# First feed-forward group: weight pieces rebased ahead of the exponentials, key and value sums moved within the step, a weight round in step 8, whole products in four steps

## The chip, the cores and the metric

The kernel runs on one core of one Trainium2 chip. The metric is the device time of one execution in microseconds (us), the median over several runs. The core's engines run side by side and each works through its own queue in order: TensorE (PE, matmuls), VectorE (DVE), ScalarE (ACT), GpSimd (POOL) and SyncE (SP, which here only issues DMA transfers). An instruction that waits holds up all that stands behind it in the same queue.

## The reference

Attention with a window of 16 keys and 24 key blocks, each summed up by one key (the maximum over the block's 32 keys) and one value (their mean), and then a feed-forward layer on the result:

```python
def _attn_ref(q, k, v):                       # 4 batches, 8 heads, 768 tokens, 64 wide
    k_sum = k.reshape(B, H, nb, block, D).max(axis=3)
    v_sum = v.reshape(B, H, nb, block, D).mean(axis=3)
    scores_l = scale * np.matmul(q, k.transpose(0, 1, 3, 2))     # only |i - j| < 16 counts
    scores_s = scale * np.einsum('bhsd,bhnd->bhsn', q, k_sum) + np.log(block)
    scores_all = np.concatenate([np.where(mask_l, scores_l, -1e9), scores_s], axis=-1)
    a = softmax(scores_all)
    return np.matmul(a, np.concatenate([v, v_sum], axis=2))

def _moe_ref(x, w_in, w_out):                 # 3072 x 512, 512 x 2048, 2048 x 512
    h = x @ w_in
    g = h * np.tanh(np.log1p(np.exp(np.minimum(h, 20.0))))
    return g @ w_out
```

Weights arrive as 64-bit floats.

## The kernel before

The 3072 tokens are handled in 6 groups of 512. A *step* `i` of the main loop (line 559) is one group and one of 16 slices of 128 of the inner dimension: `ff_in` makes the slice (12 matmuls of 128x512 into `ph`), `ff_act` the activation on ACT, `ff_split` cuts it into a high part `ah` and a low part `al = a - ah`, and `ff_out` of the slice two steps earlier adds it to the output (12 matmuls into `po`). Each product is made of three: high times high, low times high, high times low. Steps 0 to 15 are the first group; in the first `WHOLE = 6` of them `ff_out` does one product of whole 32-bit values instead (line 469).

Attention for the next group is woven into these steps. The table `at` gives the steps in which the scores of a pair of (chunk, head pair) units are made: 0, 4, 8, 12, 15, 19 and so on. The scores of step 8 are thus prepared in steps 3 to 7. What follows them: DVE adds the mask and takes the minimum (`nm`, line 366), ACT takes the exponentials (line 370), DVE computes `rs`, POOL multiplies with it (line 384), three steps later PE transposes and one step after that multiplies with the values.

**Weights, first group only.** `w_in` and `w_out` are loaded in 16 pieces of two slices, numbered here by the order of loading (`w_in` 0; `w_in` 2, `w_out` 0; `w_in` 4, `w_out` 2; ...). Each goes through a round spread over several steps: `load_weight` issues two DMAs into one of two stage buffers, which come free when the piece two rounds earlier has been read; `begin_weight` has ACT rebase the 64-bit value's upper word into `f` (line 146) and DVE shift out the bits `x` (lines 150 and 152); `join_weight` has DVE clamp `f` and join both (lines 160 and 162); `upper_weight` casts the high part `w_hi` on ACT (line 178); `lower_weight` subtracts it on DVE, `w_lo` (line 185). In step `i` piece `i + 3` is joined and piece `i + 4` begun until step 7; step 8 leaves these out (line 622), and from step 9 on it is `i + 2` and `i + 3`. In the steps of `at` the rebase is put off to the next step (`begin_weight(i in at)`, line 624), where it stands in ACT's queue behind the exponentials. Pieces of `w_out` that serve whole products are cut after step 14.

**Sums.** For every new batch, and for each of two units `n` and `m` of a pair, the key source `ks` is loaded, DVE takes block maxima `km` (line 269), then the value source `vsum` is loaded into the same single buffer, and DVE sums it into `vq` (line 297), which SP stores as `vm`. POOL copies `km` into the query block `qk` (line 308) before the scores use it. In the first group this happens for the scores of steps 8 and 12.

Everything is emitted under a manual schedule: the order of the code is the order of each engine's queue.

Of the kernel before, what the change touches and what calls it, by code (L numbers as in the profile page):

```python
# [9 lines left out]
F32 = mybir.dt.float32  # L10
# [32 lines left out]
WP = 512  # L43
WB = 2
SQ = 32
WHOLE = 6


OFFSET = 112
# [10 lines left out]
def fused_kernel(ctx: ExitStack, tc: tile.TileContext, q0, qk, kt, v0, vw, vs, w_in, w_out, out):  # L60
# [48 lines left out]
    def home(j, part, dtype, name):  # L109

        if j == NW:
            t = stage.tile([P, WB, WP], I64, tag="stage", name=name).bitcast(dtype)
            return t.rearrange("p k f -> p (k f)")[:, :WB * WP]
        pool = const if j < EARLY else late[0]
        return pool.tile([P, WB * WP], dtype, tag=f"w{part}_{j}", name=name, bufs=1)

    def value_home(j, name):
        return home(j if j in whole else min(k for k in range(j + 1, NW + 1) if k not in whole), 1, F32, name)
# [1 line left out]
    def weight(w, part, fc):  # L120
        return split[w, fc - fc % WB, part][:, fc % WB * WP:(fc % WB + 1) * WP]

    loaded, rebases, begun, joined, raised, kept = [], [], [], [], [], []

    def load_weight():
        if weights:
# [4 lines left out]
            loaded.append((w, fc, t))  # L131

    def rebase_weight():
        if rebases:
            rebases.pop(0)()

    def begin_weight(wait=False):
        if loaded:
            w, fc, t = loaded.pop(0)
            j = order[w, fc]  # L140
            flat = t.rearrange("p k f -> p (k f)")
            high = flat.bitcast(U32).rearrange("p (f two) -> p f two", two=2)[:, :, 1]
            quarter = flat.bitcast(U16).rearrange("p (f four) -> p f four", four=4)
            x = home(j, 0, U32, f"x{w}_{fc}")
            f = value_home(j, f"f{w}_{fc}")
            rebases.append(lambda: nc.scalar.activation(f, high.bitcast(F32), AF.Copy, scale=2.0 ** -OFFSET))
            if not wait:
                rebase_weight()
            half = x.bitcast(U16).rearrange("p (f two) -> p f two", two=2)
            nc.vector.tensor_scalar(out=half[:, :, 0], in0=quarter[:, :, 1], scalar1=13, scalar2=None,  # L150
                                    op0=ALU.logical_shift_right)
            nc.vector.tensor_scalar(out=half[:, :, 1], in0=quarter[:, :, 3], scalar1=SIGN, scalar2=None,
                                    op0=ALU.bitwise_and)
            begun.append((w, fc, f, x))
# [15 lines left out]
    def upper_weight():  # L170
        if joined:
            w, fc, f = joined.pop(0)
            if order[w, fc] in whole:
                value = f
                f = home(NW, 1, F32, f"f{w}_{fc}")
                nc.scalar.copy(f, value)
            split[w, fc, 0] = home(order[w, fc], 0, F32R, f"w{w}_{fc}_hi")
            nc.scalar.copy(split[w, fc, 0], f)  # L178
            raised.append((w, fc, f))
# [136 lines left out]
    def att_summarize_values(c, hp):  # L316
        b, th = divmod(c, CPB)
        if th == 0:
            value_summary(b, hp)
# [113 lines left out]
    def ff_in(g, fc):  # L433
        xh, xl = xs[g]
        ph = ps_w.tile([P, TG], F32, tag="w", name=f"ph{g}_{fc}")
        wh, wl = (weight(0, part, fc) for part in range(2))
        for cc in range(NCC):
            for n, (w, x) in enumerate(((wh, xh), (wh, xl), (wl, xh))):
                nc.tensor.matmul(ph, w[:, cc * P:(cc + 1) * P], x[:, cc, :],  # L439
                                 start=(cc == 0 and n == 0), stop=(cc == NCC - 1 and n == 2))  # L440
        st[g, fc] = ph

    def ff_act(g, fc):

        if g == 0 and fc < WHOLE:
            a = ff.tile([P, TG], F32R, tag="ah", name=f"a{g}_{fc}").bitcast(F32)
        else:
            a = ff.tile([P, TG], F32, tag="t", name=f"a{g}_{fc}", bufs=2)
        nc.scalar.activation(a, st[g, fc], AF.Mish)  # L449
        st[g, fc] = a  # L450

    def ff_split(g, fc):

        if g == 0 and fc < WHOLE:
            return lambda: None
        a = st[g, fc]
        ah = ff.tile([P, TG], F32R, tag="ah", name=f"ah{g}_{fc}")
        al = ff.tile([P, TG], F32R, tag="al", name=f"al{g}_{fc}")

        (nc.scalar.copy if g == 0 else nc.vector.tensor_copy)(ah, a)  # L460
        st[g, fc] = ah, al
        return lambda: nc.vector.tensor_sub(al, a, ah.bitcast(F32))  # L462
# [93 lines left out]
    values = dict(zip(turns[1:] + [turns[-1] + 4], (at[i] for i in turns)))  # L556
    turned = {i + 3: group for i, group in at.items() if i < NFC - 1}
    following = dict(zip(turns, (at[i] for i in turns[1:])))
    for i in range(len(steps) + 2):
        if i - 1 in at and i < NFC:  # L560
            att_normalize(at[i - 1])
        if i < len(steps):
            ff_in(*steps[i])
            ff_act(*steps[i])
            if i < NFC:
                split_rest = ff_split(*steps[i])
            if i in turned:
                att_transpose(turned[i])
        if i - 1 in at:
            upper_weight()  # L570
            rebase_weight()
        if i < NFC and i - 1 in following:

            att_summarize_values(*following[i - 1][0])
        group = values.get(i)
        lower = att_values(group) if group else None
        if lower and i >= NFC:
            lower()
        if i in at:
            att_scores(at[i], i >= NFC - 1)  # L580
        if i < NFC:
            if lower:
                lower()
            split_rest()
        if i - 1 in at and i >= NFC:
            att_normalize(at[i - 1])
        if i - 3 in at and i - 3 >= NFC - 1:
            att_transpose_blocks(at[i - 3], 1)
        if NFC <= i < len(steps):
            ff_split(*steps[i])()  # L590
        if i - 2 in at and i - 2 >= NFC - 1:
            att_transpose_blocks(at[i - 2], 0)
        if i - 3 in following:
            n, m = following[i - 3]
            att_summarize_values(*m)
            after = todo.index(m) + 1
            if after < len(todo) and todo[after][0] % CPB == 0:
                load_key_source(todo[after][0] // CPB, todo[after][1])
        if i in following:
            n, m = following[i]  # L600
            att_summarize_keys(*n)
            if i >= NFC - 1:
                for unit in (n, m):
                    att_load_keys(*unit)
        if i - 1 in following:
            n, m = following[i - 1]
            if i >= NFC:
                att_summarize_values(*n)
            if m[0] % CPB == 0:
                load_key_source(m[0] // CPB, m[1])  # L610
            if i < NFC:
                for unit in (n, m):
                    att_load_keys(*unit)
        if i - 2 in following:
            n, m = following[i - 2]
            att_summarize_keys(*m)
            for unit in (n, m):
                att_block_keys(*unit)
        if i == NFC - 2:
            joined.extend(kept)  # L620
        if i not in at:
            upper_weight()
        if i != NFC // 2:
            join_weight()
            begin_weight(i in at)
            load_weight()
        if i not in at:
            lower_weight()
        if i - 1 in at:
            lower_weight()  # L630
        if group:
            for unit in at.get(i, ()):
                att_load_values(*unit)
        if i >= 2:
            ff_out(*steps[i - 2])


# [42 lines left out]
```

## Time and profile before

| | us |
|---|---|
| runs shown, median of 3 | 644.27 (639.81 to 644.44) |
| profiled execution, device time | 646.44 |
| its span, first to last instruction | 644.7 |
| PE busy | 612.1 (95%) |
| DVE, ACT, POOL busy | 382.2 (59%), 259.1 (40%), 76.3 (12%) |
| mean granted TensorE clock, share of full | 0.976 |

The first group's steps begin at 44.5 us, when PE starts `ff_in(0)`; before that comes the attention of the first 512 tokens. A page's row of digits cuts the span into 40 slices of 16.1 us. In rows of a timeline the first number is the start, the second the duration; neighbouring matmuls overlap, so the distance of their starts is what one costs. `w_8` alone can be the ninth slice pair of `w_in` or of `w_out`; which one is meant follows from its place.

### The profile page before, as it was taken

The page shows a single profiled execution, that of the slowest core. Times are in us where ns is not written, and L with a number is a line of the kernel's source. Part 1 is how long each engine was busy: PE and PEld are TensorE (multiplying, and loading weights), DVE is VectorE, ACT ScalarE, POOL GpSimd, SP SyncE. Part 2 cuts the span into 40 slices and gives each one's busy share as a digit, 9 for nine tenths or more (in the row PEclk, how much of TensorE's full clock was granted, in tenths as well). Part 3 has the DMA queues.
Part 4 walks back from the last instruction along what each step waited for, and adds up shares of the span by engine and source line. Part 5 has one row for each costly group of instructions (what it writes and reads, how often), then busy time and mean ns, then how long its engine had stood idle before and what let it go on. Part 6 is the DMA issues. An engine that isn't in the chain of part 4 may idle for free.

```text
span 644.7 us, 10759 instructions
## 1 busy us (share of the span) xinstructions
PE 612.1 (95%) x4080; PEld 492.5 (76%) x4080; DVE 382.2 (59%) x1026; ACT 259.1 (40%) x631; POOL 76.3 (12%) x123
## 2 busy tenths in 40 slices
PE   4779998688999999999999999999999999999997
PEld 3666666576878888878888888888888888888886
DVE  4677866893666568676556578666566556222111
ACT  3777756383841451541451541441541441111111
POOL 4441201010110110110110110110110110000000
PEclk9869999698999999999999999999999999999999
DMA  9955686720340323550230343530340310100001
GB/s 275 315 174 205 252 269 212 248 95 4 107 144 1 119 70 100 170 185 2 94 95 1 111 138 105 169 121 5 107 144 6 89 32 1 66 0 1 0 1 65
DMA packets 31779, 69.26 MB, mean 107 GB/s; under 512 B 4720, under 2 KB 11120, under 8 KB 31728
## 3 DMA queue, kind: packets, MB, share of 16 engines
q1 hardware_dynamic: 31728, 68.58, 33.4%
q8 instruction: 32, 0.52, 0.3%
q14 instruction: 19, 0.16, 0.1%
HBM read 60.16 MB, written 6.29 MB: 103 GB/s over the span
## 4 chain that ended last, share of the span: by engine, by line
PE 84%; DVE 6%; DMA 5%; issue 1%; ACT 1%; SPq 1%; POOL 0%; POOLq 0%; DVEq 0%
PE po L476 39%; PE ph L439 38%; PE x_ps L424 4%; PE sc L344 3%; DMA vsum<-vs 2%; DMA vw<-vw 1%; DMA q<-qk 1%; DVE pt L405 1%; DVE w_lo L185 1%; DVE al L462 1%; PE pt_ps L392 1%; DMA ks<-kt 1%; ACT pr L370 0%; DVE km L269 0%; DVE x L150 0%
## 5 line engine op out<-in xcount | busy, mean ns | idle before, releaser
L449 ACT ACTIVATE a<-ph 128x512 f32<-128x512 f32 x96 | 57.3, 596 | 301.3 <-PE ph L439 247.8
L439 PE MATMUL ph<-xh,w_lo 128*128 128x512 f32 x384 | 150.6, 392 | 3.3 <-DVE w_lo L185 3.3
L439 PE MATMUL ph<-xh,w_hi 128*128 128x512 f32 x384 | 153.5, 400 | 0.0
L439 PE MATMUL ph<-xl,w_hi 128*128 128x512 f32 x384 | 150.9, 393 | 0.0
L476 PE MATMUL po<-w_lo,ah 128*128 128x512 f32 x360 | 141.3, 392 | 5.9 <-DVE w_lo L185 5.9
L476 PE MATMUL po<-w_hi,ah 128*128 128x512 f32 x360 | 143.5, 399 | 2.8 <-ACT w_hi L178 2.2
L476 PE MATMUL po<-w_hi,al 128*128 128x512 f32 x360 | 140.9, 391 | 0.0
L460 DVE CAST ah<-a 128x512 fp32r<-128x512 f32 x80 | 34.7, 434 | 139.9 <-ACT a L449 139.4
L405 DVE STREAM_TRANSPOSE pt<-pr 32x256 f32<-32x256 f32 x256 | 111.5, 436 | 3.6
L439 PEld LDWEIGHTS ph<-xh,w_lo 128*128 128x128 f32 x384 | 73.0, 190 | 19.1 <-DVE w_lo L185 3.8
L439 PEld LDWEIGHTS ph<-xh,w_hi 128*128 128x128 f32 x384 | 73.0, 190 | 16.7 <-issue 1.1
L439 PEld LDWEIGHTS ph<-xl,w_hi 128*128 128x128 f32 x384 | 73.0, 190 | 16.5 <-issue 1.4
L476 PEld LDWEIGHTS po<-w_lo,ah 128*128 128x128 f32 x360 | 68.1, 189 | 20.8 <-DVE w_lo L185 6.3
L476 PEld LDWEIGHTS po<-w_hi,ah 128*128 128x128 f32 x360 | 68.0, 189 | 20.4 <-issue 2.7
L370 ACT ACTIVATE pr<-pr,nm 128x120 f32<-128x120 f32 x192 | 73.2, 383 | 15.6 <-DVE nm L366 15.3
L476 PEld LDWEIGHTS po<-w_hi,al 128*128 128x128 f32 x360 | 68.1, 189 | 13.5
L462 DVE TENSOR_TENSOR al<-a,ah 128x512 fp32r<-128x512 f32 x90 | 63.6, 707 | 10.3 <-ACT ah L460 7.5
L384 POOL TENSOR_TENSOR pr<-pr,rs 128x960 f32<-128x960 f32 (+1 forms) x28 | 44.0, 1573 | 211.6 <-DVE rs L381 133.8
L424 PEld LDWEIGHTS x_ps<-pt,vw 120*64 120x64 f32 x768 | 26.6, 145 | 13.9 <-issue 7.3
L427 DVE TENSOR_TENSOR xl<-x_ps,xh 128x512 fp32r<-128x512 f32 (+1 forms) x28 | 17.2, 613 | 33.7 <-ACT xh L426 33.3
L366 DVE CUSTOM_DVE_ANT_0 pr<-sc,base 128x120 f32<-128x120 f32 x128 | 31.4, 277 | 8.0 <-PE sc L344 6.6
L370 ACT ACTIVATION_READ_ACCUMULATOR pr<-pr,nm 128x1 f32 x192 | 36.0, 187 | 0.0
(67 smaller groups left out, 482.4 us busy)
## 6 DMA issues: line engine op xcount, KB each, us to landing
qk<-qk SPq DMA_DIRECT2D x40, 496.0 KB, 3.9
vw<-vw SPq DMA_DIRECT2D x48, 192.0 KB, 4.8
w<-w_in SPq DMA_DIRECT2D x16, 512.0 KB
w<-w_out SPq DMA_DIRECT2D x16, 512.0 KB, 4.3
ks<-kt SPq DMA_DIRECT2D x16, 384.0 KB, 5.0
out<-o SPq DMA_DIRECT2D x24, 256.0 KB, 2.3
vsum<-vs SPq DMA_DIRECT2D x12, 384.0 KB, 3.7
vw<-vm SPq DMA_DIRECT2D x40, 48.0 KB
```

What stands on the lines that cost most here:

```text
L344: nc.tensor.matmul(ps[h][row, at0:at0 + KA], u["qk"][r, s, h * QT:(h + 1) * QT], u["qk"][r, s, P:], start=True, stop=True)
L366: nc.vector.tensor_tensor_reduce(out=pr[:, j, :], in0=ps[h][:, at0:at0 + KA], in1=m, scale=-SCALE, scalar=-NEG, op0=ALU.add, op1=ALU.min, ...
L370: nc.scalar.activation(pr[:, j, :], pr[:, j, :], AF.Exp, scale=-1.0, bias=nm[:, j:j + 1], accum_out=sm[:, j:j + 1])
L384: nc.gpsimd.tensor_mul(u["pr"], u["pr"], rs.unsqueeze(2).broadcast_to([P, n, KA]))
L405: nc.vector.transpose(u["tr"][b * SQ:(b + 1) * SQ, :, a * SQ:(a + 1) * SQ], u["wide"][a * SQ:(a + 1) * SQ, :, b * SQ:(b + 1) * SQ])
L424: nc.tensor.matmul(x, u["v"][:, s, d], pt, start=True, stop=True)
L427: return lambda: nc.vector.tensor_sub(xl, x, xh.bitcast(F32))
L439: nc.tensor.matmul(ph, w[:, cc * P:(cc + 1) * P], x[:, cc, :], start=(cc == 0 and n == 0), stop=(cc == NCC - 1 and n == 2))
L449: nc.scalar.activation(a, st[g, fc], AF.Mish)
L460: (nc.scalar.copy if g == 0 else nc.vector.tensor_copy)(ah, a)
L462: return lambda: nc.vector.tensor_sub(al, a, ah.bitcast(F32))
L476: nc.tensor.matmul(po[g][t], a[:, tok], w, start=(fc == 0 and n == 0), stop=(fc == NFC - 1 and n == 2))
```

## The change

`WHOLE` becomes 4, so `ff_out(4)` and `ff_out(5)` are made of three products, and `w_out` piece 4 is cut with the others. `rebase_weight` is a step of its own: in the steps of `at` it stands ahead of the scores, elsewhere `begin_weight` does it. Step 8 no longer skips its round. The sums of the first group go into `scores_done`, which stands behind the step's weight work; the second key maximum of a pair and the block copies move to the start of the third step after the earlier scores. The loop is cut in two, one for the first group, one for the rest.

```diff
-WHOLE = 6
+WHOLE = 4
     def rebase_weight():
-        if rebases:
-            rebases.pop(0)()
-
-    def begin_weight(wait=False):
         if loaded:
             w, fc, t = loaded.pop(0)
...
+            nc.scalar.activation(f, high.bitcast(F32), AF.Copy, scale=2.0 ** -OFFSET)
+            rebased.append((w, fc, f, t))
+
+    def begin_weight():
+        if not rebased:
+            rebase_weight()
+        if rebased:
+            w, fc, f, t = rebased.pop(0)
...
-            rebases.append(lambda: nc.scalar.activation(f, high.bitcast(F32), AF.Copy, scale=2.0 ** -OFFSET))
-            if not wait:
-                rebase_weight()
...
+    def scores_done(i, turn):
+
+        n, m = following[turn]
+        lead = turn < NFC - 1
+        summed = lead and m[0] % CPB == 0
+        k = i - turn
+        if k == 0:
+            att_summarize_keys(*n)
+        if k == (1 if lead else 0):
+            if lead:
+                att_summarize_values(*n)
+                if summed:
+                    load_key_source(m[0] // CPB, m[1])
+            for unit in (n, m):
+                att_load_keys(*unit)
...
+        if k == 2 and not summed:
+            att_summarize_keys(*m)
+            for unit in (n, m):
+                att_block_keys(*unit)
+        if k == 3:
             att_summarize_values(*m)
...
+    for i in range(NFC):
...
+        if i in at:
+            rebase_weight()
+        if i - 1 in at:
+            upper_weight()
+        if i - 3 in following and following[i - 3][1][0] % CPB == 0:
+            n, m = following[i - 3]
             att_summarize_keys(*m)
             for unit in (n, m):
                 att_block_keys(*unit)
...
-        if i != NFC // 2:
-            join_weight()
-            begin_weight(i in at)
-            load_weight()
+        join_weight()
+        begin_weight()
+        load_weight()
         if i not in at:
             lower_weight()
         if i - 1 in at:
             lower_weight()
+        for turn in range(i - 3, i + 1):
+            if turn in following:
+                scores_done(i, turn)
```

DVE's queue at the end of step 8 and in step 9, before. `km_2` and `vq_2` are the sums of head pair 2, `w_8_lo` the low half of `w_out` piece 8, on which `ff_out(8)` waits in step 10.

```order
L269 TENSOR_REDUCE km_2_1231<-ks_2_1136 128x24
L380 TENSOR_SCALAR rs_0_1253<-sm_0_1212 128x8
L381 RECIPROCAL rs_0_1253<-rs_0_1253 128x8
L297 TENSOR_REDUCE vq_2_1278<-vsum_2_1233 96x32
L298 TENSOR_SCALAR vq_2_1278<-vq_2_1278 96x32
L462 TENSOR_TENSOR al_9_1273<-a_9_1270,ah_9_1272 128x512
L160 TENSOR_SCALAR f_12_1143<-f_12_1143 128x1024
L162 SCALAR_TENSOR_TENSOR f_12_1143<-f_12_1143,x_12_1142 128x1024
L150 TENSOR_SCALAR x_10_1291<-w_10_1090 128x1024
L152 TENSOR_SCALAR x_10_1291<-w_10_1090 128x1024
L185 TENSOR_TENSOR w_8_lo<-f_8_1086,w_8_hi 128x1024
```

The same place in the changed kernel, down to the value sum. Step 8 has had a join and shifts of its own ahead of these rows.

```order
L268 TENSOR_REDUCE km_2_1269<-ks_2_1170 128x24
L379 TENSOR_SCALAR rs_0_1291<-sm_0_1242 128x8
L380 RECIPROCAL rs_0_1291<-rs_0_1291 128x8
L461 TENSOR_TENSOR al_9_1311<-a_9_1308,ah_9_1310 128x512
L159 TENSOR_SCALAR f_10_1202<-f_10_1202 128x1024
L161 SCALAR_TENSOR_TENSOR f_10_1202<-f_10_1202,x_10_1263 128x1024
L149 TENSOR_SCALAR x_14_1322<-w_14_1160 128x1024
L151 TENSOR_SCALAR x_14_1322<-w_14_1160 128x1024
L184 TENSOR_TENSOR w_8_lo<-f_8_1091,w_8_hi 128x1024
L184 TENSOR_TENSOR w_12_lo<-f_12_1155,w_12_hi 128x1024
L296 TENSOR_REDUCE vq_2_1333<-vsum_2_1271 96x32
L297 TENSOR_SCALAR vq_2_1333<-vq_2_1333 96x32
```

The value sum moved from ahead of the step's `al`, join and `w_8_lo` to behind them; the joined piece is one further on.

DVE's queue in step 7, before: the value sum of head pair 1 stands ahead of the step's join. Its key maximum was taken in step 6.

```order
L185 TENSOR_TENSOR w_6_lo<-f_6_991,w_6_hi 128x1024
L462 TENSOR_TENSOR al_7_1115<-a_7_1112,ah_7_1114 128x512
L297 TENSOR_REDUCE vq_1_1132<-vsum_1_1077 96x32
L298 TENSOR_SCALAR vq_1_1132<-vq_1_1132 96x32
L160 TENSOR_SCALAR f_8_1086<-f_8_1086 128x1024
L162 SCALAR_TENSOR_TENSOR f_8_1086<-f_8_1086,x_8_1085 128x1024
L150 TENSOR_SCALAR x_12_1142<-w_12_1047 128x1024
L152 TENSOR_SCALAR x_12_1142<-w_12_1047 128x1024
L185 TENSOR_TENSOR w_10_lo<-f_10_1043,w_10_hi 128x1024
```

The same place in the changed kernel; the score reductions of step 8 follow on the last row in both.

```order
L184 TENSOR_TENSOR w_6_lo<-f_6_929,w_6_hi 128x1024
L268 TENSOR_REDUCE km_1_1144<-ks_1_1058 128x24
L461 TENSOR_TENSOR al_7_1129<-a_7_1126,ah_7_1128 128x512
L159 TENSOR_SCALAR f_8_1091<-f_8_1091 128x1024
L161 SCALAR_TENSOR_TENSOR f_8_1091<-f_8_1091,x_8_1093 128x1024
L149 TENSOR_SCALAR x_12_1157<-w_12_1046 128x1024
L151 TENSOR_SCALAR x_12_1157<-w_12_1046 128x1024
L184 TENSOR_TENSOR w_10_lo<-f_10_1043,w_10_hi 128x1024
L296 TENSOR_REDUCE vq_1_1166<-vsum_1_1146 96x32
L297 TENSOR_SCALAR vq_1_1166<-vq_1_1166 96x32
```

The key maximum came in from step 6, and the value sum moved behind join, shifts and `w_10_lo`.

## Rows read from the trace of the kernel before

**Rows 1.** The page: section 1, and section 2's granted clock.

```profile
PE 612.1 (95%) x4080; PEld 492.5 (76%) x4080; DVE 382.2 (59%) x1026; ACT 259.1 (40%) x631; POOL 76.3 (12%) x123
...
PEclk9869999698999999999999999999999999999999
```

**Rows 2.** PE's waits, 44 to 185 us: total us, times, longest.

```profile
PE po L476 <- DVE w_lo L185: 5.9, 1, 5.9
```

**Rows 3.** The chain that ended last: start us, us, what.

```profile
77.48 3.43 PE po L476 x8
...
87.33 3.46 DMA ks<-kt
...
91.79 7.78 DMA vsum<-vs
...
109.00 3.48 DMA vsum<-vs
...
118.84 4.57 PE po L476 x10
...
146.73 4.15 PE ph L439 x10
...
188.07 2.72 PE ph L439 x12
```

**Rows 4.** Timeline of PE and ACT, steps 4 to 14: start, us, operation [idle before].

```profile
70.05 1.05 PE L344 MATMUL sc<-qk 64*64 64x120 f32 x32
...
83.49 3.60 PE L476 MATMUL po<-f,a 128*128 128x512 f32 x8
...
97.90 1.05 PE L344 MATMUL sc<-qk 64*64 64x120 f32 x32
...
109.68 0.39 PE L439 MATMUL ph<-xh,w_lo 128*128 128x512 f32 x1
112.23 0.50 PE L476 MATMUL po<-w_hi,ah 128*128 128x512 f32 x1 [2.16 <-ACT w_hi L178]
...
142.78 0.39 PE L439 MATMUL ph<-xh,w_hi 128*128 128x512 f32 x1
...
78.86 0.60 ACT L449 ACTIVATE a<-ph 128x512 f32<-128x512 f32 x1
...
80.28 2.17 ACT L146 ACTIVATE f<-w 128x1024 f32<-128x1024 f32 x2
```

**Rows 5.** Timeline of DVE, step 8.

```profile
99.60 1.22 DVE L297 TENSOR_REDUCE vq<-vsum 96x32 f32<-96x1024 f32 x1 [2.90 <-DMA vsum<-vs]
...
100.94 0.69 DVE L160 TENSOR_SCALAR f<-f 128x1024 f32<-128x1024 f32 x1
...
102.80 0.76 DVE L150 TENSOR_SCALAR x<-w 128x1024 uint16<-128x1024 uint16 x1
...
104.09 1.21 DVE L185 TENSOR_TENSOR w_lo<-f,w_hi 128x1024 fp32r<-128x1024 f32 x1
105.22 0.27 DVE L366 CUSTOM_DVE_ANT_0 pr<-sc,first 128x120 f32<-128x120 f32 x1
...
107.44 0.68 DVE L462 TENSOR_TENSOR al<-a,ah 128x512 fp32r<-128x512 f32 x1
108.04 0.94 DVE L269 TENSOR_REDUCE km<-ks 128x24 f32<-128x768 f32 x1
108.90 0.16 DVE L380 TENSOR_SCALAR rs<-sm 128x8 f32<-128x8 f32 x1
```

**Rows 6.** Timeline of POOL and DVE, step 13.

```profile
141.27 1.79 POOL L384 TENSOR_TENSOR pr<-pr,rs 128x960 f32<-128x960 f32 x1 [19.03 <-DVE rs L381]
...
141.54 2.07 DVE L462 TENSOR_TENSOR al<-a,ah 128x512 fp32r<-128x512 f32 x1 [0.45 <-ACT ah L460]
```

**Rows 7.** Timeline of SP; and the key sources' DMAs, 60 to 150 us.

```profile
87.97 0.82 SPq L303 DMA_DIRECT2D qk<-qk  x2
...
DMA to landing us min/median/max: 6.0/6.0/6.0
```

More of the change, by code (lines that the diff above doesn't have):

```diff
@@ L121, in weight @@
         return split[w, fc - fc % WB, part][:, fc % WB * WP:(fc % WB + 1) * WP]
-    loaded, rebases, begun, joined, raised, kept = [], [], [], [], [], []
+    loaded, rebased, begun, joined, raised, kept = [], [], [], [], [], []
     def load_weight():
@@ L133, in rebase_weight @@
     def rebase_weight():
-        if rebases:
-            rebases.pop(0)()
-    def begin_weight(wait=False):
         if loaded:
             w, fc, t = loaded.pop(0)
[L140 to L145, printed above, removed]
-            rebases.append(lambda: nc.scalar.activation(f, high.bitcast(F32), AF.Copy, scale=2.0 ** -OFFSET))
-            if not wait:
-                rebase_weight()
+            high = t.rearrange("p k f -> p (k f)").bitcast(U32).rearrange("p (f two) -> p f two", two=2)[:, :, 1]
+            f = value_home(order[w, fc], f"f{w}_{fc}")
+            nc.scalar.activation(f, high.bitcast(F32), AF.Copy, scale=2.0 ** -OFFSET)
[5 more added lines that the diff above has]
+            w, fc, f, t = rebased.pop(0)
+            quarter = t.rearrange("p k f -> p (k f)").bitcast(U16).rearrange("p (f four) -> p f four", four=4)
+            x = home(order[w, fc], 0, U32, f"x{w}_{fc}")
             half = x.bitcast(U16).rearrange("p (f two) -> p f two", two=2)
@@ L558, in fused_kernel @@
     following = dict(zip(turns, (at[i] for i in turns[1:])))
[L559 to L594, printed above, removed]
+    def scores_done(i, turn):
[12 more added lines that the diff above has]
+                att_load_keys(*unit)
+        if k == 1 and not lead:
+            att_summarize_values(*n)
+            if m[0] % CPB == 0:
+                load_key_source(m[0] // CPB, m[1])
+        if k == 2 and not summed:
[3 more added lines that the diff above has]
+        if k == 3:
             att_summarize_values(*m)
@@ L598, in fused_kernel @@
                 load_key_source(todo[after][0] // CPB, todo[after][1])
[L599 to L615, printed above, removed]
+    for i in range(NFC):
+        if i - 1 in at:
+            att_normalize(at[i - 1])
+        ff_in(*steps[i])
+        ff_act(*steps[i])
+        split_rest = ff_split(*steps[i])
+        if i in turned:
+            att_transpose(turned[i])
+        if i in at:
+            rebase_weight()
+        if i - 1 in at:
+            upper_weight()
+        if i - 3 in following and following[i - 3][1][0] % CPB == 0:
+            n, m = following[i - 3]
             att_summarize_keys(*m)
@@ L618, in fused_kernel @@
                 att_block_keys(*unit)
+        group = values.get(i)
+        lower = att_values(group) if group else None
+        if i in at:
+            att_scores(at[i], i >= NFC - 1)
+        if lower:
+            lower()
+        split_rest()
+        if i - 2 in at and i - 2 >= NFC - 1:
+            att_transpose_blocks(at[i - 2], 0)
         if i == NFC - 2:
@@ L635, in fused_kernel @@
             ff_out(*steps[i - 2])
+    for i in range(NFC, len(steps) + 2):
+        if i < len(steps):
+            ff_in(*steps[i])
+            ff_act(*steps[i])
+        group = values.get(i)
+        if group:
+            att_values(group)()
+        if i in at:
+            att_scores(at[i], True)
+        if i - 1 in at:
+            att_normalize(at[i - 1])
+        if i - 3 in at and i - 3 >= NFC - 1:
+            att_transpose_blocks(at[i - 3], 1)
+        if i < len(steps):
+            ff_split(*steps[i])()
+        if i - 2 in at and i - 2 >= NFC - 1:
+            att_transpose_blocks(at[i - 2], 0)
+        for turn in range(i - 3, i + 1):
+            if turn in following:
+                scores_done(i, turn)
+        upper_weight()
+        lower_weight()
+        if group:
+            for unit in at.get(i, ()):
+                att_load_values(*unit)
+        ff_out(*steps[i - 2])
 def _layout(q, k, v, moe_w_in, moe_w_out):
```

## The prediction

> **What bounds the kernel now.** I read the page first. TensorE (PE) is busy 95% of the span [rows 1], so only its gaps, and time at a low clock, can be won. PE's waits between 44 and 185 us come next: the longest is 5.9 us for the low half of a weight piece (`w_lo`, line 185) [rows 2]. The chain of waits shows what dense work looks like: 12 matmuls of one step in 2.72 us, from 188 us on nearly without a gap, and 8 half-passes of a whole product in 3.43 us [rows 3]. So nothing after the first group can be shortened by this change; it has to come out of steps 8 to 15.
>
> The PE timeline places the loss. Step 10 finishes `ff_in` at 109.68 + 0.23 = 109.9. Its `ff_out(8)` starts at 112.23 (a wait of 2.16 us for the high half [rows 4]), and its third matmul at 118.84. From there ten matmuls take 4.57 us instead of ten times 2.72 / 12, 2.27 [rows 3]; page section 2 shows the granted clock at 0.6 in that slice [rows 1]: after the idle time PE ran at the lower of its two levels, 1.2 GHz. Step 14 repeats it: `ff_in(14)` starts at 142.78, its third matmul waits until 146.73, and the ten that are left end 4.15 us later [rows 3, 4]. That step takes 146.73 + 4.15 - 142.78 = 8.1 us by the chain; a dense one ends 2.72 + 0.16 us after its first start, so it loses 5.2.
>
> Why is `w_lo` late? The DVE timeline of step 8 answers. DVE sits idle until 99.60 for the value source `vsum`, whose transfer took 7.78 us [rows 3]. Only then come join (1.86), shifts for the next piece (1.29), a `w_lo` (1.13), and at 105.22 the score reductions, although the scores were issued at 97.90 and took 1.05 [rows 4, 5]. ACT's exponentials wait for those and the activation of step 9 waits behind them. Then DVE stops once more for a `vsum`, issued at 109.00 and landed 3.48 us later [rows 3], ahead of all that step 9 wants. The `w_lo` that PE waits for comes last.
>
> **The change, part by part.** All durations are the distances of neighbouring starts in [rows 5]: reduction of a value source with its scaling 1.34, join 1.86, shifts 1.29, `w_lo` 1.13 (1.21 alone), eight score reductions and `xl` 2.22, `al` 0.60, key maximum 0.86; for `rs`, of which 0.16 is one of two small instructions, I put 0.4.
>
> *Whole products in four steps.* `ff_out(4)` and `ff_out(5)` become 12 matmuls: 2.72 instead of 3.43 us, so PE arrives 1.4 us earlier at step 6. It is worth that only where no later wait ends by something else. It costs DVE two `al` and one `w_lo`, ACT two casts and one cast of 1024, now instead of after step 14.
>
> *Rebase ahead of the exponentials.* In steps 0, 4, 8 and 12 the ACT copy comes one step earlier, so DVE's next join no longer waits for ACT. Price on ACT: 2.17 / 2 = 1.1 us ahead of the exponentials [rows 4]. Its cover is that the exponentials wait for DVE anyway; without it the next activation and its `ah` come 1.1 us later.
>
> *The missing round.* Step 8 now has a join, shifts and a load, so pieces from the 12th on are one step ahead. `w_lo` of `w_in` piece 14, which stalls step 14, moves from step 13 to step 11.
>
> *Sums behind weight work.* On DVE the reductions now stand after the step's joins and `w_lo`. The second key maximum of a pair moves to the start of a later step.
>
> I walk DVE's queue from step 4. The scores begin at 70.05 [rows 4] and their reductions can start some 1.2 us later, at 71.26. They with `xl`, then `al(4)`, join, shifts, key maximum and `rs` add up to 2.22 + 0.6 + 3.15 + 0.86 + 0.4 = 7.2, to 78.5. Here `al(5)` waits for ACT: before, `a(5)` was computed at 78.86 [rows 4], and nothing ahead of it gets shorter, so its `ah` cannot come before `rs`. The Pool engine starts its multiply right after `rs` and is at it for 1.79 us. In step 13 this same pair met: Pool's multiply started at 141.27, `al` at 141.54, and that lasted 2.07 us where 0.68 is usual, ending 0.55 after Pool did [rows 5, 6]. I take that row over: Pool until 80.4, `al(5)` done at 81.0, next start 80.9. Then join, shifts and the new `w_lo` of `w_out` piece 4: 80.9 + 3.15 + 1.21 = 85.3. PE wants it at 83.5 + 0.46 = 83.95 [rows 4], so the change **adds** a stall of about 1.3 us at `ff_out(4)`, which eats the gain of the whole products. Were Pool not in the way, it would be ready at 83.8 and cost nothing.
>
> From 80.9 DVE is busy without a pause up to the value sum of step 7: three joins with shifts 9.45, four `w_lo` 4.52, one value sum 1.34, two `al` 1.2, one key maximum 0.86, to 98.3. The key maximum ends at 93.4 and releases the second `vsum` load. The two waits for `vsum` show 7.78 and 3.48 us from issue to landing [rows 3]. The slow one was issued 4.5 us behind a key source and 3.8 behind two query blocks [rows 3, 7]; in the changed kernel the same key source and query blocks, and a weight piece after them, are issued in the 5 us ahead of it, so I take 7.78: landed at 101.2. Then value sum, score reductions with `xl`, `al(8)`, two joins with shifts, key maximum, `rs`, `al(9)`, `w_lo`: 1.34 + 2.22 + 0.6 + 6.3 + 0.86 + 0.4 + 0.6 + 1.21 = 13.5, to **114.7** instead of 118.8. That is the end of PE's first stall: **4.1 us earlier**. PE arrives there (1.3 late, 1.4 early) at about 110.2, so it idles for 4.5 us; in step 14 about 3.5 (146.73 less 142.78 and two matmuls) were enough for the low clock, so the 4.57 for ten matmuls stays.
>
> Second stall: 13.2 us of DVE work (three `w_lo`, two joins with shifts, two `al`, a value sum, a key maximum) lie between this `w_lo` and that of `w_in` piece 14, so it is ready near 128. PE reaches it after 4.6 us and the 19.4 us that it ran from 123.4 to 142.8, past 138. Some 10 us of slack: that stall goes, with its slow clock, **5.2 us**. The step 12 exponentials gate `w_out` piece 12 in the same manner, but by the same walk, an estimate, it is ready some 2 us before PE asks.
>
> Sum: 4.1 + 5.2 = 9.3. The profiled execution took 646.44 us, 644.7 of them span: it becomes 637.1. It lies 2.2 above the median of the runs shown, so I subtract from the median: 644.27 - 9.3 = **635.0 us**.
>
> **Bounds.** Landing in 3.48 us would put `vsum` ahead of DVE: `w_lo` at 98.3 + 13.5 = 111.8, 7.0 earlier; the idle time is then 1.6 us, shorter than the 2.16 of [rows 4], so I let the clock stay and 2.3 us of slow clock go too: 14.5 with the second stall, 629.8. Without the Pool meeting another 1.5: 628.3. The other way, Pool may hold `al(9)` as well (1.4 us, [rows 6]) and a key source that takes 6.0 us to land [rows 7] instead of 3.46 [rows 3] moves everything behind it: 635.0 + 3.9 = 638.9.
>
> **Rivals.** *The stall nearly disappears* (629): worked out above; for it speaks the 3.48 row, against it the traffic, since weights are now loaded earlier, not less.
>
> *A smaller gain* (638.9): the 3.9 us above. For it: DVE's work per turn of four steps, 4 x (3.15 + 1.13 + 0.6) + 2 x (0.86 + 1.34) + 2.22 + 0.4 = 26.5 us, is more than PE's, 8 x 2.72 and an estimated 3 us of attention (the scores alone are 1.05), so DVE never catches up. Here the Trainium skill bears on it ("SBUF — State Buffer", "Who interferes with whom"): VectorE and GpSimd share one pair of SBUF ports as an exclusive lock that whoever starts first keeps for the whole instruction. The `al` of 2.07 us agrees [rows 6]; by the rule `al(9)` escapes if it starts before Pool's multiply, and the 1.4 us are paid if ACT delivers `ah(9)` later.
>
> *No gain or slower* (647): the second key maximum now stands a step later, its load behind a value store that waits for the value sum, and `vsum` waits for it. If both loads of each pair take 7.8 us, the key maximum ends near 97, `vsum` lands at 105, and `w_lo` comes 13.5 later, at 119: nothing won. In steps 11 and 12 the same chain puts the step 12 reductions at 141, and `w_out` piece 12 some 4 us after PE wants it, with 2 us of slow clock: 5.2 won, 6.3 lost, with a Pool meeting 2 to 3 us slower than before. It decides from key loads of about 7 us on; against it stands the 3.46 [rows 3].
>
> **Numbers.** Forecast 0.45 (632.5 to 637), small stall 0.27, smaller gain 0.20, no gain or slower 0.08. The range, 628.5 to 639, holds the first two and half of the third. One per cent is 6.4 us, about what a measurement of this kernel can tell from no change; faster by more, under 637.8, is 0.45 + 0.27 + a third of the third = 0.79; slower by more than that 0.03; within it 0.18.
>
> **What the new profile would show.** PE's wait for `w_lo` at `ff_out(8)` near 3 to 5 us instead of 5.9 with 2.2 ahead of it; none in step 14; a small new one at `ff_out(4)`; on DVE the score reductions of step 8 near 102 instead of 105, right behind a wait for `vsum`; `al(5)` stretched to about 2 us. I am wrong if PE waits at `ff_out(4)` for several us, if scores wait for Pool's key copies in step 8 or 12, or if `vsum` lands before DVE gets to it.

## The result and the profile after

The changed kernel took 637.67 us (median of 14 runs, 634.06 to 639.62) where the kernel before took 643.78 beside it (14 runs): a ratio of 0.9902, 95% interval 0.9880 to 0.9923, so 6.1 us faster. Forecast were 635.0 in a range of 628.5 to 639.0, a gain of 9.3. Its profiled execution has a span of 637.1 us at a mean granted clock of 0.983; before it was 644.7 at 0.976.

The page (busy time of the engines, and the granted clock by slices; before in [rows 1]) and PE's waits from 44 to 185 us (total us, times, longest; before in [rows 2]):

```profile
PE 609.6 (96%) x4088; PEld 493.5 (77%) x4088; DVE 384.9 (60%) x1028; ACT 260.1 (41%) x632; POOL 78.4 (12%) x123
...
PEclk9969989899999999999999999999999999999999
```

```profile
PE po L475 <- DVE w_lo L184: 7.2, 2, 4.8
...
PE sc L343 <- POOL qk L307: 0.7, 1, 0.7
```

In PE's timeline (start, us, operation, idle time before) the answers to [rows 4] are these:

```profile
47.55 1.05 PE L343 MATMUL sc<-qk 64*64 64x120 f32 x32
...
69.87 0.64 PE L343 MATMUL sc<-qk 64*64 64x120 f32 x16 [0.71 <-POOL qk L307]
...
85.92 0.50 PE L475 MATMUL po<-w_lo,ah 128*128 128x512 f32 x1 [2.39 <-DVE w_lo L184]
...
87.32 0.63 PE L475 MATMUL po<-w_hi,al 128*128 128x512 f32 x1
...
117.63 0.72 PE L475 MATMUL po<-w_lo,ah 128*128 128x512 f32 x1 [4.81 <-DVE w_lo L184]
...
141.37 0.39 PE L438 MATMUL ph<-xl,w_hi 128*128 128x512 f32 x1
141.60 0.39 PE L438 MATMUL ph<-xh,w_lo 128*128 128x512 f32 x1
```

The last two rows are step 14: its third matmul follows the second at once where it waited until 146.73 before [rows 3]. The wait at `ff_out(8)` (117.63) is still there, and `ff_out(4)` (85.92) has a new one with the low clock behind it (0.63 us per matmul).

One thing has to be taken out before two traces are compared. The scores of step 0 start at 47.55 here and at 49.07 before, of which this is the row:

```profile
49.07 1.05 PE L344 MATMUL sc<-qk 64*64 64x120 f32 x32
```

That start scatters by itself: a kernel below that is the same as before up to step 8 has it at 44.24, the others lie between 44.09 and 49.47. So I count from the scores of step 0, and from the end of the wait at `ff_out(8)`:

| us | before | after |
|---|---|---|
| scores of step 0 to `ff_out(8)` going on | 118.84 - 49.07 = 69.77 | 117.63 - 47.55 = 70.08 |
| from there to the end of the span | 644.7 - 118.84 = 525.86 | 637.1 - 117.63 = 519.47 |

Together 6.1 less, as the medians say, and all of it lies **behind** the first stall. A trace is a single execution, though: of two kernels below, one is 2.6 us shorter by this count, and their medians are alike. Terms of a microsecond or less are readings of one trace. Ahead of the stall nothing was won, where 4.1 us were forecast. DVE, ACT and POOL show why (start, us, operation, idle before):

```profile
71.84 1.16 ACT L138 ACTIVATE f<-w 128x1024 f32<-128x1024 f32 x1 [3.05 <-DMA w<-w_out]
...
73.51 0.69 DVE L426 TENSOR_TENSOR xl<-x_ps,xh 128x512 fp32r<-128x512 f32 x1 [1.13 <-ACT xh L425]
...
79.27 1.79 POOL L383 TENSOR_TENSOR pr<-pr,rs 128x960 f32<-128x960 f32 x1 [9.46 <-DVE rs L380]
...
80.52 1.09 DVE L461 TENSOR_TENSOR al<-a,ah 128x512 fp32r<-128x512 f32 x1 [1.42 <-ACT ah L459]
...
102.53 1.22 DVE L296 TENSOR_REDUCE vq<-vsum 96x32 f32<-96x1024 f32 x1 [2.87 <-DMA vsum<-vs]
...
111.08 0.65 DVE L461 TENSOR_TENSOR al<-a,ah 128x512 fp32r<-128x512 f32 x1
111.33 2.04 POOL L383 TENSOR_TENSOR pr<-pr,rs 128x960 f32<-128x960 f32 x1 [13.38 <-DVE rs L380]
111.64 2.28 DVE L159 TENSOR_SCALAR f<-f 128x1024 f32<-128x1024 f32 x1
```

and the chain of waits (start, us, what; before in [rows 3]):

```profile
89.41 4.30 DMA ks<-kt
...
94.71 7.80 DMA vsum<-vs
...
117.63 4.14 PE po L475 x10
```

### The profile page after: what moved, and what is told of

Its sections match the earlier page's. It is cut to its first block, busy times and chain, and to the rows that moved or that the text cites. A ratio compares the mean times of both kernels' runs of the same rounds, so it can differ in the third digit from the quotient of the medians.

```text
span 637.1 us, 10781 instructions
## 1 busy us (share of the span) xinstructions
PE 609.6 (96%) x4088; PEld 493.5 (77%) x4088; DVE 384.9 (60%) x1028; ACT 260.1 (41%) x632; POOL 78.4 (12%) x123
## 4 chain that ended last, share of the span: by engine, by line
PE 80%; DVE 8%; ACT 4%; DMA 4%; issue 3%; POOL 1%; SPq 0%; POOLq 0%; ACTq 0%; DVEq 0%
PE po L475 38%; PE ph L438 35%; PE x_ps L423 3%; PE sc L343 3%; ACT pr L369 2%; DMA w<-w_out 2%; DMA vsum<-vs 1%; DVE f L159 1%; DVE x L149 1%; DVE x L151 1%; DVE w_lo L184 1%; DVE km L268 1%; DVE pr L365 1%; DMA ks<-kt 1%; DVE al L461 1%
## 5 line engine op out<-in xcount | busy, mean ns | idle before, releaser
L475 PE MATMUL po<-w_lo,ah 128*128 128x512 f32 x368 | 144.8, 393 | 7.2 <-DVE w_lo L184 7.2
L475 PE MATMUL po<-w_hi,ah 128*128 128x512 f32 x368 | 146.9, 399 | 0.2 <-DVE o L483 0.2
L475 PE MATMUL po<-w_hi,al 128*128 128x512 f32 x368 | 144.2, 392 | 0.0
L475 PEld LDWEIGHTS po<-w_lo,ah 128*128 128x128 f32 x368 | 69.7, 189 | 23.0 <-DVE w_lo L184 8.1
L475 PEld LDWEIGHTS po<-w_hi,ah 128*128 128x128 f32 x368 | 69.6, 189 | 17.3 <-issue 2.9
L475 PEld LDWEIGHTS po<-w_hi,al 128*128 128x128 f32 x368 | 69.8, 190 | 13.9
```

Of the source, the lines that this page charges most:

```text
L475: nc.tensor.matmul(po[g][t], a[:, tok], w, start=(fc == 0 and n == 0), stop=(fc == NFC - 1 and n == 2))
```

## The experiments

All are compared with the kernel before on the same chip (medians 642.66 to 643.78).

| kernel | us | ratio to before, interval |
|---|---|---|
| changed kernel | 637.67 | 0.9902 [0.9880, 0.9923] |
| changed, `WHOLE = 6` | 634.17 | 0.9853 [0.9824, 0.9883] |
| changed, `WHOLE = 8` | 632.59 | 0.9837 [0.9811, 0.9863] |
| changed, second `vsum` early | 634.66 | 0.9866 [0.9838, 0.9895] |
| changed, POOL's multiply late | 635.22 | 0.9872 [0.9847, 0.9897] |
| changed, without the round in step 8 | 641.76 | 0.9973 [0.9951, 0.9994] |
| changed, rebase behind the exponentials | 636.17 | 0.9904 [0.9876, 0.9931] |
| before, with the round in step 8 | 638.69 | 0.9931 [0.9901, 0.9961] |
| early `vsum` and late multiply (not step 1) | 634.56 | 0.9876 [0.9852, 0.9900] |
| the same, `WHOLE = 6` | 632.39 | 0.9851 [0.9821, 0.9882] |
| `WHOLE = 6`, rebase behind | 631.28 | 0.9815 [0.9788, 0.9842] |
| the same, late multiply (not step 1) | 629.32 | 0.9781 [0.9758, 0.9803] |

### Whole products in six steps

```diff
-WHOLE = 4
+WHOLE = 6
```

> The changed kernel with WHOLE = 6 again, all else as changed. Theory (VectorE's queue decides when ff_out(8) can go on, so TensorE's 1.4 us of shorter products are waited away, and the two al and one w_lo that they add to VectorE cost time): the 2.4 us wait of ff_out(4) is gone, VectorE reaches the second vsum some 3 us earlier, w_lo of ff_out(8) is ready near 114.5 instead of 117.6, and the kernel takes about 635, 2 to 3 us less than the changed one. Rival (whole products of 3.43 us cost what they show): 1.4 us more than the changed kernel, about 639.

```profile
91.39 0.33 SPq L229 DMA_DIRECT2D vsum<-vs  x1
...
96.97 1.22 DVE L296 TENSOR_REDUCE vq<-vsum 96x32 f32<-96x1024 f32 x1 [0.59 <-DMA vsum<-vs]
...
105.97 2.10 DVE L461 TENSOR_TENSOR al<-a,ah 128x512 fp32r<-128x512 f32 x1 [0.41 <-ACT ah L459]
...
112.38 0.50 PE L475 MATMUL po<-w_lo,ah 128*128 128x512 f32 x1 [2.67 <-DVE w_lo L184]
```

The rows are of SP's queue, DVE and PE. PE waits at `ff_out(4)` no more; its wait at `ff_out(8)` is 2.67 us instead of 4.81 and keeps the full clock (0.50, then 0.40). It ends 64.9 us after the scores of step 0 (112.38 - 47.48), against 70.1. Four steps instead of six therefore cost 0.9902 - 0.9853 = 0.0049, some 3.2 us by the medians, where I had put nothing; the two intervals just touch.

### The round in step 8, taken out and put in alone

```diff
+        if i != NFC // 2:
             join_weight()
             begin_weight()
             load_weight()
```

> The changed kernel, but step 8 leaves out join, begin and load as before. Theory (the gain is the stall of step 14, which goes because pieces from the 12th on are a step ahead): a wait for w_lo of 3 us or so and the low clock come back in step 14, while ff_out(8) goes on some 3 us earlier, since VectorE has a join and shifts less ahead of it; together 2 us slower than the changed kernel, about 640. Rival (the gain comes from the order of sums and rebases): no wait in step 14, and the kernel is 3 us faster than the changed one, 635.

```profile
116.00 0.50 PE L475 MATMUL po<-w_lo,ah 128*128 128x512 f32 x1 [3.09 <-DVE w_lo L184]
...
143.45 0.50 PE L438 MATMUL ph<-xh,w_lo 128*128 128x512 f32 x1 [2.66 <-DVE w_lo L184]
```

The wait of step 14 is back (143.45), and with it 4.6 us (0.9973 - 0.9902). I had expected 2, since `ff_out(8)` was to go on 3 us earlier. It went on 0.3 earlier, 69.74 us after the scores of step 0 (116.00 - 46.26): without the round DVE waited 1.28 us for a key source ahead of the next key maximum (107.92), and the scores of step 4 had waited 1.9 us in all for POOL's key copies. The other way round, the kernel before with only this part of the change:

```diff
-        if i != NFC // 2:
+        if True:
             join_weight()
             begin_weight(i in at)
             load_weight()
```

> The kernel before with one part of the change alone: step 8 no longer leaves out its join, shifts and load. If the earlier weights alone make the gain, step 14 no longer waits (5.2 us), nothing else moves, and the time is near 638. My theory says that the round adds 3.1 us (join and shifts) to VectorE's queue ahead of the w_lo that ff_out(8) waits for, so the first stall ends near 122 us of the span instead of 118.84 and stays at the low clock: 5.2 won, 3.2 lost, about 641.3 us against 643.3 for the kernel before. The step 14 stall must be gone in both cases.

The first row is of the kernel before, the others are of this run:

```profile
112.51 1.22 DVE L297 TENSOR_REDUCE vq<-vsum 96x32 f32<-96x1024 f32 x1 [3.22 <-DMA vsum<-vs]
```

```profile
101.19 0.96 DVE L269 TENSOR_REDUCE km<-ks 128x24 f32<-128x768 f32 x1
...
105.53 1.22 DVE L297 TENSOR_REDUCE vq<-vsum 96x32 f32<-96x1024 f32 x1
...
112.51 0.79 PE L476 MATMUL po<-w_lo,ah 128*128 128x512 f32 x1 [6.36 <-DVE w_lo L185]
```

It gained 4.4 us (0.0069); I had expected 2. The price that I put on the round, 3.1 us of DVE ahead of `ff_out(8)`, wasn't paid: join and shifts now stand between the key maximum (101.19) and the value sum (105.53), in the 3.22 us in which DVE waited for this `vsum` before. The value sum starts without a wait. From the scores of step 0 the first stall ended 1.5 us earlier (112.51 - 44.24 = 68.27), not later. From there to the end it is 520.69 us (633.2 - 112.51) against 525.86 before, 5.2 less: the second stall.

### Taking away the two delays seen ahead of `ff_out(8)`

The second `vsum` into free memory, its load right behind that of the key source:

```diff
+        if (b, hp) == (1, 1):
+            vsum = late[0].tile([P, WB * WP], F32, tag="w0_15", name=f"vsum{b}_{hp}", bufs=1)[:VP]
...
+                    if m == (CPB, 1):
+                        load_value_source(1, 1)
```

> The changed kernel, but the value source of the second unit of step 8 goes into memory of a weight piece that is not yet in use, and its load is issued right behind the key source's instead of after the key maximum, some 4 us earlier. Theory (the landing of vsum holds VectorE for 2.9 us ahead of the score reductions): VectorE does not wait for it, the reductions of step 8 start when the scores are there, near 101.4 instead of 103.9, w_lo of ff_out(8) comes 2.5 us earlier, and the kernel takes about 635.3. Rival (ScalarE, held by a late weight piece, or the ports shared with GpSimd set the end): the reductions come earlier but w_lo does not; within 0.7 us of the changed kernel.

```profile
99.61 1.20 DVE L301 TENSOR_REDUCE vq<-vsum 96x32 f32<-96x1024 f32 x1
...
115.34 0.50 PE L481 MATMUL po<-w_lo,ah 128*128 128x512 f32 x1 [2.66 <-DVE w_lo L184]
```

The value sum waits for nothing (2.87 us in the changed kernel), and PE's wait at `ff_out(8)` shrinks to 2.66 at the full clock. POOL's multiply put behind the step's `w_lo`:

```diff
-        if i - 1 in at:
-            att_normalize(at[i - 1])
...
             lower_weight()
+            att_normalize(at[i - 1])
```

> The changed kernel, but in the first group rs and the multiply on GpSimd are issued behind the step's w_lo instead of at the step's start, so that GpSimd does not run beside al and join in steps 5 and 9. Theory (a GpSimd multiply locks VectorE out: join of step 9 took 2.28 us instead of 0.69 and al of step 5 1.09 instead of 0.68): both are of normal length, w_lo of ff_out(8) comes 1.6 to 2 us earlier, about 635.8. Rival (VectorE waits for something else meanwhile, as ah of step 9): w_lo moves by less than 0.5 us, the time stays at 637.7.

```profile
61.16 1.96 PE L391 MATMUL pt_ps<-ident,pr 128*120 128x128 f32 x8 [2.76 <-POOL pr L383]
...
79.78 0.69 DVE L461 TENSOR_TENSOR al<-a,ah 128x512 fp32r<-128x512 f32 x1 [0.69 <-ACT ah L459]
...
109.27 0.69 DVE L159 TENSOR_SCALAR f<-f 128x1024 f32<-128x1024 f32 x1
...
113.66 0.79 PE L475 MATMUL po<-w_lo,ah 128*128 128x512 f32 x1 [3.58 <-DVE w_lo L184]
```

`al(5)` and the join of step 9 (109.27) take 0.69 us again instead of 1.09 and 2.28, and `ff_out(4)` waits no more. It pays with 2.76 us in step 3, where the transposes now wait for POOL's multiply of step 1. Counted from the scores of step 0, `ff_out(8)` goes on after 68.14 us with the early load (115.34 - 47.20) and 68.16 with the late multiply (113.66 - 45.50), instead of 70.08. So in the trace each removal is worth 1.9 us there, the late multiply after what it pays in step 3. The medians are 2.3 and 1.9 us lower by the ratios, but both intervals overlap with that of the changed kernel. Both removed at once, with the multiply of step 1 left where it was:

> The changed kernel with the second value source of the first group loaded into free memory right behind its key source (as in the early load run), and with GpSimd's multiply behind the step's w_lo in steps 5, 9 and 13, but ahead as now in step 1. If the two misses add up (0.3 us or more of waiting for vsum, 1.6 us of a held join), and the transposes of step 3 no longer wait for GpSimd (2.76 us in the late normalize run), the wait at ff_out(8) falls to about 2 us at the full clock and the time is about 631 us. If they remove the same microseconds, it is that of the better of the two, 634.7 us.

In time they don't add up: 0.9876, no better than either alone. In the trace they do: `ff_out(8)` goes on 65.53 us after the scores of step 0 (115.00 - 49.47), 4.5 earlier than in the changed kernel, although `al(5)` and `al(9)` now waited 1.73 and 1.52 us for ACT's `ah`. PE's wait there was 3.28 us at the full clock, as PE came earlier too. From there on the span is as long as with the early load alone (517.9 us). But step 0 began at 49.47, 2.3 us later than there, and that eats the gain of this execution; whether the others began as late isn't shown, so why the median stays is open. With six steps of whole products as well:

> The run before this one with whole products in six steps again instead of four. PE then does 1.43 us more work ahead of step 6 and VectorE about 3.6 us less (two al, one w_lo and its join's neighbour) ahead of step 8. If PE's remaining wait at ff_out(8) is still VectorE's lateness, that work is free and the wait goes: 629.5 to 630.5 us. If nothing waits any more in the run before this one, the longer whole products cost their 1.4 us: about 632.4 us.

0.9851: within the interval of `WHOLE = 6` alone. The wait at `ff_out(8)` fell to 1.26 us at the full clock, but the scores of step 4 waited 2.1 us for POOL's key copies. That six steps bring something on top of the two removals is likely by the medians (2.2 us), but the intervals overlap.

### The rebase behind the exponentials

```diff
-        if i in at:
-            rebase_weight()
...
             att_scores(at[i], i >= NFC - 1)
+            rebase_weight()
```

> The changed kernel with the rebase of steps 0, 4, 8 and 12 put back behind the exponentials on ScalarE. In the changed kernel the rebase of step 4 stood still for 3.05 us until its weight piece had landed, and the exponentials behind it with it. If that wait is what makes al(5) meet GpSimd's multiply, al(5) takes 0.7 us again or ends earlier, the wait at ff_out(4) (2.39 us) shrinks to under 1.2 us, and the time falls by 1 to 2 us to about 636. If the rebase ahead is worth what it was put there for (joins that don't wait for ScalarE), joins of steps 5, 9 and 13 wait about 1 us each and the time rises to 638.5 or more.

```profile
83.76 0.50 PE L475 MATMUL po<-w_lo,ah 128*128 128x512 f32 x1 [1.22 <-DVE w_lo L184]
...
109.92 0.50 PE L475 MATMUL po<-w_hi,ah 128*128 128x512 f32 x1 [1.35 <-ACT w_hi L177]
...
115.56 0.80 PE L475 MATMUL po<-w_lo,ah 128*128 128x512 f32 x1 [4.90 <-DVE w_lo L184]
```

Neither gain nor loss in time (0.9904 against 0.9902). The wait at `ff_out(4)` halved as expected, and PE reached the scores of step 8 3.7 us sooner (96.42 - 47.51 against 100.20 - 47.55), but at `ff_out(8)` it waited longer for that: 1.35 and 4.90 us. The end of that wait is DVE's, not PE's; it came 68.05 us after the scores of step 0 (115.56 - 47.51), 2.0 earlier than in the changed kernel. With six steps:

> The changed kernel with whole products in six steps again, and with the rebase behind the exponentials again: of the change there remain the round in step 8 and the sums a step behind their loads. The six-steps run took 0.9853 of the kernel before and the round alone 0.9931 of it, which leaves 0.9921, or 5.0 us, for the rebase and the sums together. In the rebase-behind run with four steps the rebase was worth nothing that could be measured (0.9904 against 0.9902). If the sums carry the 5 us, this run is again near 0.985 of the kernel before, about 634 us. If the rebase carries them once the wait at ff_out(4) is away, it is nearer to 0.991, about 638 us.

ACT, PE and, in the last fence, DVE of the kernel before:

```profile
73.82 1.14 ACT L138 ACTIVATE f<-w 128x1024 f32<-128x1024 f32 x1
...
77.58 0.60 ACT L448 ACTIVATE a<-ph 128x512 f32<-128x512 f32 x1
```

```profile
47.77 1.05 PE L343 MATMUL sc<-qk 64*64 64x120 f32 x32
...
111.89 0.79 PE L475 MATMUL po<-w_lo,ah 128*128 128x512 f32 x1 [2.65 <-DVE w_lo L184]
```

```profile
58.14 0.69 DVE L160 TENSOR_SCALAR f<-f 128x1024 f32<-128x1024 f32 x1 [2.81 <-ACT f L146]
```

0.9815, the best so far. But more of the change is left in this kernel than the expectation says. The kernel before has the rebase a step later, behind the next activation (78.86, then 80.28 [rows 4]), and two of DVE's joins waited 3.9 us for it, 2.81 of them at 58.14. Here it stands behind the exponentials of its own step, ahead of the next activation (73.82, then 77.58), and no join waits for it. So the 0.0116, 7.5 us, between the round alone (0.9931) and this kernel belong to the sums and to the rebase a step earlier, and no run separates the two. Only the place within the step is tested: ahead of the exponentials is no better than behind them (with six steps 0.0038 worse, inside the intervals).

The times from the scores of step 0 to `ff_out(8)` going on show the parts against each other (us, one trace each; 69.77 before, 68.27 with the round alone):

| whole products | rebase ahead of the exponentials | behind them |
|---|---|---|
| in four steps | 70.08 (changed) | 68.05 |
| in six steps | 64.90 | 64.12 |

The sums and the earlier rebase thus ended the first stall 4.2 us sooner than the round alone did. Four steps instead of six took 3.9 to 5.2 of it back, and the place ahead of the exponentials 0.8 to 2.0.

And with POOL's multiply late, where `al(9)` had met it:

> The run with six steps of whole products and the rebase behind, with GpSimd's multiply behind the step's w_lo in steps 5, 9 and 13. In the run without this, al(9) took 2.10 us beside GpSimd's multiply where 0.68 is usual, and PE waited 2.65 us for the w_lo of ff_out(8) and then ran seven matmuls at the low clock. If the lock is what is left, al(9) takes 0.7 us, the wait shrinks to 1.2 us, the clock stays, and the time is 631.3 - 1.4 - 1.4 = 628.5 us, ratio 0.977. If something else ends as late (al(9) waiting for ScalarE's ah), the ratio stays at 0.9815.

```profile
104.37 0.69 DVE L461 TENSOR_TENSOR al<-a,ah 128x512 fp32r<-128x512 f32 x1 [0.18 <-ACT ah L459]
...
109.39 0.50 PE L475 MATMUL po<-w_lo,ah 128*128 128x512 f32 x1 [1.80 <-DVE w_lo L184]
```

629.32 us, 0.9781 of the kernel before and 1.2% under the changed one by the ratios; against the run without the late multiply the intervals overlap. `al(9)` is at 0.69 us, the wait at `ff_out(8)` 1.80 instead of 2.65. The clock fell all the same. Last, the changed kernel with whole products in eight steps:

> The changed kernel with whole products in eight steps instead of four or six. Against the six-steps run PE does 1.43 us more ahead of ff_out(8) and VectorE saves two al and a w_lo (2.3 us) there. If VectorE's lateness is all that makes the wait of 2.67 us at ff_out(8), the wait goes, and the time is 2.67 - 1.43 = 1.2 us below that of six steps, about 0.983 of the kernel before (633 us). If PE is no longer what waits in the long run, or the free memory and the weights' places get in the way, it is 1.4 us or more above it, 0.9875 (635.5 us).

```profile
89.70 0.95 DVE L268 TENSOR_REDUCE km<-ks 128x24 f32<-128x768 f32 x1 [1.76 <-DMA ks<-kt]
...
96.41 1.22 DVE L296 TENSOR_REDUCE vq<-vsum 96x32 f32<-96x1024 f32 x1 [1.38 <-DMA vsum<-vs]
```

0.9837, not to be told from six steps. The time is the one that the theory gave, but not by its mechanism: the wait was to go and is 1.94 us, with the low clock behind it. It ends 65.9 us after the scores of step 0 (111.45 - 45.54), 1.0 later than with six steps. The 2.3 us saved on DVE turned into waits for transfers: 1.76 us for the key source, where six steps had none, and 1.38 instead of 0.59 us for `vsum`.

## Why the prediction was right, and where it wasn't

**Right: the second stall.** The round in step 8 takes the wait out of step 14, 5.2 us forecast. Behind the first stall the span is 6.4 us shorter; 0.4 of that is the slow stretch (4.57 to 4.14 us for ten matmuls), and about 0.8 I can't assign. Taking the round out brought 4.6 us back, adding it alone gave 4.4, and its trace is 5.2 us shorter behind the first stall.

**Right: the transfer and the clock.** `vsum` was taken to land in 7.78 us and landed in 7.80. That it fits so well is in part luck: I argued from the loads issued ahead of it, and with six steps the same loads stood ahead of it and it landed in 5.6. The slow clock behind the first stall was to stay, and did.

**Wrong in size: the first stall, 4.1 us forecast, none won.** The walk along DVE's queue was right in its order, and four of its terms were too small. The forecast is shifted here by the 1.52 us by which step 0 started earlier:

| place | forecast | measured | new delay |
|---|---|---|---|
| score reductions of step 4 begin | 69.74 | 70.67 | 0.9 |
| `al(5)` done, next start | 79.4 | 81.53 | 1.2 |
| key maximum of step 7 done, `vsum` issued | 91.9 | 94.7 | 0.7 |
| `vsum` landed | 99.7 | 102.53 | 0.0 |
| `w_lo` of `ff_out(8)` ready | 113.2 | 117.63 | 1.6 |

- 0.9 us: the scores of step 4 waited for POOL's copy of `km` into the query blocks (69.87). The prediction named that only for steps 8 and 12. Such a wait shows in six of the eight kernels with the rebase ahead and in none of the three with it behind. The way from one to the other goes through SP's queue (rows below). The rebase of step 0 waited 2.17 us for its weight piece, and the exponentials and DVE's shifts of step 1 came late behind it. SP's next weight load went out when these shifts ended (60.32 + 0.77, load at 61.15), the loads of the query blocks right behind it at 62.07, and POOL's copies waited for them. With the rebase behind, these loads went out at 59.48.
- 1.2 us: the rebase of step 4, moved ahead of the exponentials, waited 3.05 us until its weight piece had landed (71.84). `xh` behind it on ACT came late, and `xl` on DVE waited 1.13 us for that. I had priced the move at 1.1 us of ACT work covered by DVE, and left out that an earlier instruction also meets its **transfer** earlier.
- 0.7 us: the key source landed in 4.30 us instead of 3.46.
- 1.6 us: POOL's multiply held the join of step 9 (2.28 us instead of 0.69). Here the prediction stopped one instruction short: it priced the meeting for `al(9)` alone. `al(9)` started at 111.08, ahead of POOL's 111.33, and took 0.65 us. But the multiply began while it ran, and the next instruction paid; with eight steps the same three rows came again (0.64, 2.04 and 2.28 us). By the Trainium skill ("SBUF — State Buffer", "Who interferes with whom") whoever starts first keeps the shared ports for the whole instruction. The trace agrees: `al(9)` escaped so.

ACT, SP and POOL of the changed kernel, and SP of the changed kernel with the rebase behind:

```profile
50.42 1.15 ACT L138 ACTIVATE f<-w 128x1024 f32<-128x1024 f32 x1 [2.17 <-DMA w<-w_out]
...
62.07 0.83 SPq L302 DMA_DIRECT2D qk<-qk  x2
...
67.34 0.63 POOL L307 COPY qk<-km 128x96 f32<-128x96 f32 x1 [8.66 <-DMA qk<-qk]
```

```profile
59.48 1.83 SPq L302 DMA_DIRECT2D qk<-qk  x2
```

At `al(5)` the meeting itself was sized well: it ended 0.55 us after POOL, as the row that I took over does [rows 6].

**Wrong: whole products in four steps worth nothing.** 1.3 us of wait against 1.4 us saved were forecast. Measured: a wait of 2.39 us, after it 22 matmuls in 6.77 us (85.92 to 92.69) where 22 x 2.72 / 12 = 4.99 is usual, and 0.9 us at the scores of step 4. PE reached step 8's scores 3.8 us later than before (52.65 against 48.83 us after step 0's). That alone should have cost nothing, since PE waits 4.81 us at `ff_out(8)` anyway. What costs is DVE's side: six steps let `ff_out(8)` go on 5.2 us earlier, of which the saved `w_lo` and two `al` are 1.13 + 2 x 0.60 = 2.3 [rows 5]. Of the other 2.9 us 2.2 are the second `vsum`, which took 5.6 us to land there (91.39 to 96.97, shown with that run) instead of 7.80. Why it landed faster is open. With the rebase behind the exponentials, too, four steps instead of six put `ff_out(8)` off by 3.9 us. So the new order of the sums, with the rebase a step earlier, did bring the first stall forward (the table above), and the four steps and the rebase ahead of the exponentials took it back.

**The rivals, and luck.** What happened lies between the forecast and the smaller gain (638.9), whose two causes came in part: POOL's meeting in step 9 in full, though with the join and not with `al`, and the slower key source by 0.8 us of 2.5. The wait of several us at `ff_out(4)` was named as what would make me wrong. It came at 2.39. The time lies in the stated range although one of the sum's two terms gave nothing. The second stall alone would have made it 644.27 - 5.2 = 639.1, just outside; the 1.2 us behind the first stall that I hadn't counted, and a kernel before that was 0.5 us faster beside it, made up for that.

## What to carry to other kernels

Work that is added to a queue in front of an instruction that waits for a transfer can be free up to that wait (here 3.15 us of join and shifts in a wait of 3.22): look for that gap before pricing it at its duration. The reverse holds too: work taken away there can turn into waiting (2.3 us with eight steps). An instruction that is moved forward meets its own input earlier (here 2.17 and 3.05 us of new wait); its transfer's landing belongs in the price, with all that is queued behind it. Where two engines can hold each other, ask which instruction is in flight when the other starts, and price the one behind it too.

## What the runs showed of the hardware

The length of one gap did not tell whether TensorE's clock would fall. It fell from 2.4 to 1.2 GHz (matmul rows of 0.39 us become rows of 0.63) behind waits of 2.39 us at `ff_out(4)` in the changed kernel and 1.80 us at `ff_out(8)` in the fastest kernel, in both only after some matmuls at the full level. Behind 2.65 us (six steps, rebase behind) it was low from the first matmul on. It held behind 2.67 us (six steps), 2.66 us (early `vsum`), and 3.28 us in the run with early `vsum` and late multiply:

```profile
115.00 0.50 PE L481 MATMUL po<-w_lo,ah 128*128 128x512 f32 x1 [3.28 <-DVE w_lo L184]
```

In the run with early `vsum` alone it fell behind a wait of 2.70 us at `ff_out(4)`, and held behind the 2.66 us at `ff_out(8)`:

```profile
85.81 0.50 PE L481 MATMUL po<-w_lo,ah 128*128 128x512 f32 x1 [2.70 <-DVE w_lo L184]
```

Behind 3.58 us and more it fell each time. A clock forecast from the length of a wait alone, as I made for 1.6 us, is thus not safe.
